# First packs cut to 256 queries, a split weight load and 210 VectorE tiles in a gated attention kernel

## The chip, the cores and the metric

The kernel runs on one core of one Trainium2 chip. The metric is the device time of one execution in microseconds (us), taken as the median of several runs. The engines are called as the profile calls them: PE is TensorE (matrix products), PEld its weight loads, ACT is ScalarE (activations, here the exponentials), DVE is VectorE (elementwise work), POOL is GpSimd and SP is SyncE, which here issues almost all DMAs.

## What is computed

Two attention branches over the same 2048 tokens of width 512 (32 heads of 16) are mixed by a gate per token:

```python
x = A_x
g = _sigmoid((x * gate_w).sum(-1, keepdims=True))
a = _A_ref(x, A_wqkv, A_wo)
b = _B_ref(x, B_wqkv, B_w_phi, B_wo)
return g * a + (1 - g) * b
# A: softmax attention
scores = jnp.einsum("bhqd,bhkd->bhqk", q, k) * (Dh ** -0.5)
o = jnp.einsum("bhqk,bhkd->bhqd", _softmax(scores, axis=-1), v)
# B: linear attention with a feature map of both signs
phi_k = jnp.concatenate([_softmax(pk, axis=-1), _softmax(-pk, axis=-1)], axis=-1)
kv = jnp.einsum("bhsf,bhsd->bhfd", phi_k, v)
o = jnp.einsum("bhqf,bhfd->bhqd", phi_q, kv) / den
```

In B, `pk` and `pq` are k and q times a 16x16 matrix per head (`w_phi`). Branch A needs 32 x 2048 x 2048 exponentials, branch B far fewer.

## The kernel before

**Units and packs.** The scores of A are made transposed: one unit is one head, 128 keys (a key tile) and 512 queries, so a 128x512 block that fills one bank of PSUM. Four heads make a pack (`_unit`, L878): pack p is the key tile p % 16 of group p // 16. A group is four heads and one chunk of 512 queries; there are 32 groups, 512 packs, 2048 units. A unit's scores are one matmul of 32 rows by 512 columns (`_scores`, L906, L913), the four heads of a pack in the four row strips of the array. The last group alone is cut in another way (`_block`, `_parts`): its units are 4 key tiles x 128 queries.

**Who makes the exponentials.** 1840 units go to ACT (`_exp`, L954, L962): it reads a ring of five PSUM banks in turns of three and two banks (`GROUPS`), so 736 activations. The scores of turn k (`_qk`, L930) wait for the exponentials of turn k-2, and for the first two turns for `self.early`: the last reader of each bank that the first projections borrowed (bank 0 and 1: transposes of x, 2: first half of k, 3: first half of q, 4: second half of k). 208 units are taken away from ACT (`SHARES`, L766: how many in each group) and computed on DVE by bit arithmetic and a cubic (`_vector_batch`, L800; `_cubic`, L834), in batches of `NB` = 5 units; `FIRST` and `LAST` give the sizes of the first and last batches. The linear branch uses the same method on DVE (`_b_pair`, L1161). The weighted sum over keys (`_pv`, L969; `_values`, L1024, L1032) runs per pack on PE.

**The start.** `_loads` (L470) issues x in pieces (tokens 0-255, 256-511, then three times 512), the first 128 columns of the q, k and v weights of A, their rest, and then the weights of B in one DMA (`wb`, L506). x is transposed on PE (`_x_transpose`, L601) and copied out (L628). For the first 512 tokens the k and q projections are made in halves of 256 tokens (`_proj_k0` L654, evacuated at L658; `_proj_q0` L669, L675, evacuated twice at L682: once for each side of a pair of heads). The first scores need both halves of q (`b_qT[0]`). V of the first 512 tokens (`_proj_v`, L706, L715) may be made from pack 1 on.

**The linear branch.** `_b_fuse` (L1131) transposes the k part and later the q part of `WB` by DMA (L1133) into one buffer `WT`, multiplies by `wphi` (L1142) and writes the product back (L1147). Then pairs of 128-token tiles follow at due times `K0 + SK * t` for keys and `Q0 + SQ * t` for queries (L1080), in units of packs.

**What sets the order.** Nothing is ordered by hand. Every operation is put into a `Plan` (L66) with an engine, an estimated cost, a priority (`prio`, roughly the pack at which it is due) and a release (`rel`: not before that pack). `order` (L138) runs a greedy list schedule over these estimates, which gives every engine one fixed queue; `now` moves when the scores of a turn are placed, as `_qk` says:

```python
def commit(_):
    plan.now = max(plan.now, (units[-1] + 1) // 4)
```

`emit` writes the queues out with semaphore waits. Each engine then works through its queue in that order, whatever the true times are; SP's queue of DMA issues too. Where PE has room, the plan adds filling matmuls on zeros (`_fill`, L1037, L1041).

Of the kernel before, what the change touches and what calls it, by code (L numbers as in the profile page):

```python
# [10 lines left out]
P = 128  # L11
D = 512
H = 32
DH = 16
TOK = 128
# [335 lines left out]
class _Kernel:  # L351
# [118 lines left out]
    def _loads(self):  # L470
# [4 lines left out]
        self.b_WB, self.b_WoA, self.b_WoB, self.b_wphi, self.b_gw = B(), B(), B(), B(), B()  # L475
# [11 lines left out]
        def load_wa(s, part, eng, prio, lat):  # L487
# [6 lines left out]
        load_x(0, [1], 3.2)  # L494
# [16 lines left out]
    def _consts(self):  # L511
# [30 lines left out]
        self._shared_dma("wphi", parts, self.b_wphi, -5, [z])  # L542
# [3 lines left out]
    def _shared_dma(self, name, parts, buf, prio, deps, cost=0.54):  # L546
        o = self.plan.op("SP", parts, cost * len(parts), name="dma_" + name, prio=prio, deps=deps, lat=8.0)
        buf.writers = [o]


    def _projections(self):
# [3 lines left out]
        self.b_x0, self.b_k0 = [B(), B()], [B(), B()]  # L555
# [45 lines left out]
    def _x_transpose(self, j, half, bank=None):  # L601
# [5 lines left out]
        for t2 in range(2):  # L607
            t = 4 * j + 2 * half + t2
            apart = t2 and bank == 1
# [3 lines left out]
            def tr(e, t=t, t2=t2, job=job):  # L613
                bank = self._bank(job).bitcast(BF16)
                for c in range(4):
# [9 lines left out]
            def copy(e, t0=t0, n=n, job=job, k=t2 - n + 1, apart=apart):  # L625
                out = self.xT[:, :, t0 * TOK:(t0 + n) * TOK].rearrange("p c (t q) -> p t c q", t=n)
                src = self._bank(job).bitcast(BF16).rearrange("p (t c q) -> p t c q", t=2, c=4)[:, k:k + n]
                return e.activation(out, src, ACT.Copy) if apart else e.tensor_copy(out, src)  # L628
            outs.append(op("ACT" if apart else "DVE", copy, 0.5 if apart else 0.068 + 0.27 * n, deps=[mm], name="xtr_ev",
# [24 lines left out]
    def _proj_k0(self, half, bank):  # L654
# [4 lines left out]
                   self.c_dve(256), 2 * half - 2.5, -99, "kproj", [self.b_k0[half]], n=256, bank=bank)  # L659
# [9 lines left out]
    def _proj_q0(self, half, bank):  # L669
# [11 lines left out]
        for side in range(2):  # L681
# [4 lines left out]
            self.b_qT[side].writers.append(o)  # L686
        self.early[bank] = [o]
# [18 lines left out]
    def _proj_v(self, cp, j):  # L706
# [5 lines left out]
        for tt in range(4):  # L712
            def run(e, tt=tt):
                for c in range(4):
# [5 lines left out]
                    rel=due - 20 if cp else -99 if j else 1, acquire=job if tt == 0 else None)  # L720
# [177 lines left out]
    def _parts(self, u):  # L898

        p, i, kt, cp, s = self._unit(u)  # L900
        if self._block(p) is None:
            return [(kt, slice(0, QCH), slice(0, QCH))]
# [27 lines left out]
    def _qk(self, a, b):  # L930
# [19 lines left out]
        if k >= 2:  # L950
            o.slack = self.exps[k - 1]
# [507 lines left out]
```

## Time and profile before

| | |
|---|---|
| median of 3 runs | 848.72 us (848.47 to 849.05) |
| the profiled execution, its own time | 848.98 us |
| span of the profiled execution, first to last instruction | 847.2 us |
| mean granted TensorE clock | 0.999 |
| busy: ACT, DVE, PE | 834.8, 810.5, 810.2 us |
| first exponentials start, last end | 8.90 us, 842.08 us |

The profile comes from one execution. All times in it count from the first instruction of the span, so a time of the profile is smaller than the measured one by what lies around the span (1.78 us in this execution). A group or timeline row names the line of the code, the engine, the operation, output and input by name and shape, the count, and busy time; idle time before it stands with what released the engine. A timeline row starts with the start and the length in us. Activations overlap their neighbours by about a tenth of a microsecond or more, so the pitch between starts, not the length of one, is what counts.

### The profile page before, as it was taken

To read this page: it belongs to the slowest core of one execution; us is meant where nothing else is said; L and a number is where in the kernel's file an instruction comes from. 1 tells how busy PE (TensorE), PEld (TensorE's weight loads), DVE (VectorE), ACT (ScalarE), POOL (GpSimd) and SP (SyncE) were. 2 spreads that over 40 slices of the span, in tenths; PEclk is the share of its full clock that TensorE was granted. 3 is DMA by queue.
4 is the path that set the end of the run, shared out by engine and by line. 5 is a ranking of instruction groups with operands and counts; after the bars stand their busy time and mean duration, and the time that the engine had idled before them with its cause. 6 is when DMAs were issued, how large, how long until landed. Compare 5 with 4: busy or idle time off the path is not lost.

```text
span 847.2 us, 19829 instructions
## 1 busy us (share of the span) xinstructions
PE 810.2 (96%) x8880; PEld 266.0 (31%) x8880; DVE 810.5 (96%) x1029; ACT 834.8 (99%) x741; POOL 7.3 (1%) x14
## 2 busy tenths in 40 slices
PE   9999999999999999999999999999999999999998
PEld 5323233332322322223223223223222222232344
DVE  4589999999999999999999999999999999999996
ACT  6999999999999999999999999999999999999997
POOL 3000000000000000000000000000000000000000
PEclk9999999999999999999999999999999999999999
DMA  9300000000000000002002011001011010030011
GB/s 289 58 10 5 4 2 7 2 6 3 8 2 2 7 2 6 3 2 45 2 7 39 3 24 39 14 2 38 8 36 31 6 29 17 2 57 14 2 33 33
DMA packets 44164, 18.98 MB, mean 22 GB/s; under 512 B 34864, under 2 KB 43568, under 8 KB 44080
## 3 DMA queue, kind: packets, MB, share of 16 engines
q1 hardware_dynamic: 42880, 17.40, 9.2%
q8 instruction: 69, 1.13, 0.5%
q10 hardware_dynamic: 1200, 0.33, 0.2%
q14 instruction: 15, 0.12, 0.1%
HBM read 6.31 MB, written 2.10 MB: 10 GB/s over the span
## 4 chain that ended last, share of the span: by engine, by line
ACT 90%; DVE 5%; PE 3%; DMA 1%; issue 0%; SPq 0%
ACT ET L962 90%; DVE vt L817 1%; PE ps L913 1%; DVE vu L827 1%; DMA phiT<-bq 1%; DMA xn<-in_A_x_dram 0%; DVE vf L842 0%; DVE vf L839 0%; PE ps L616 0%; PE ps L644 0%; DVE vu L843 0%; PE ps L1032 0%; DVE bq L1221 0%; DVE vt L1217 0%; PE ps L1397 0%; PE ps L715 0%
## 5 line engine op out<-in xcount | busy, mean ns | idle before, releaser
L962 ACT ACTIVATE ET<-ps 128x1536 bf16<-128x1536 f32 x736 | 832.3, 1422 | 2.7 <-PE ps L913 2.6
L913 PE MATMUL ps<-qT,kT 32*128 32x512 bf16 (+1 forms) x2240 | 319.9, 365 | 31.2 <-ACT ET L962 23.6
L1041 PE MATMUL ps<-kT,zero 128*32 128x512 bf16 (+1 forms) x3176 | 262.8, 383 | 0.0
L1032 PE MATMUL ps<-ET,V 128*32 128x512 bf16 (+1 forms) x2011 | 196.8, 365 | 0.3 <-DVE T L1061 0.3
L913 PEld LDWEIGHTS ps<-qT,kT 32*128 32x128 bf16 x2240 | 84.3, 91 | 315.1 <-ACT ET L962 239.1
L817 DVE TENSOR_SCALAR vt<-ps 128x512 uint32<-128x512 f32 x208 | 136.1, 679 | 2.2 <-PE ps L913 1.4
L827 DVE SCALAR_TENSOR_TENSOR vu<-vt,vu 128x2560 int16<-128x2560 uint32 (+2 forms) x43 | 117.2, 2726 | 0.2
L1041 PEld LDWEIGHTS ps<-kT,zero 128*32 128x32 bf16 x3176 | 69.5, 94 | 109.7 <-issue 83.2
L842 DVE TENSOR_TENSOR vf<-vf 128x2560 f16<-128x2560 f16 (+2 forms) x59 | 81.2, 1377 | 0.4
L839 DVE TENSOR_SCALAR vf<-vt 128x2560 f16<-128x2560 uint8 (+2 forms) x59 | 81.3, 1378 | 0.2
L1032 PE MATMUL ps<-vu,V 128*32 128x512 bf16 (+1 forms) x229 | 78.1, 362 | 0.0
L1032 PEld LDWEIGHTS ps<-ET,V 128*32 128x32 bf16 x2011 | 54.9, 95 | 62.2 <-issue 37.1
L843 DVE TENSOR_TENSOR vu<-vu,vf 128x2560 f16<-128x2560 f16 (+2 forms) x43 | 61.6, 1434 | 0.2
L644 PE MATMUL ps<-WB,xT 128*128 128x512 bf16 x192 | 55.1, 383 | 0.5 <-DVE vt L817 0.2
L644 PE MATMUL ps<-xT,WA 128*128 128x512 bf16 (+1 forms) x128 | 36.9, 376 | 0.1
L1217 DVE TENSOR_TENSOR vt<-bq,bsum 128x2048 uint32<-128x2048 bf16 x16 | 36.6, 2287 | 0.2
L1221 DVE SCALAR_TENSOR_TENSOR bq<-vt,bq 128x2048 int16<-128x2048 uint32 x16 | 36.5, 2283 | 0.2
L841 DVE TENSOR_SCALAR vu<-vf 128x2560 f16<-128x2560 f16 (+2 forms) x43 | 33.9, 790 | 0.1
L1061 DVE STREAM_TRANSPOSE T<-ps 128x512 f32<-128x512 f32 (+1 forms) x35 | 23.0, 657 | 3.0 <-PE ps L1032 3.0
L1032 PEld LDWEIGHTS ps<-vu,V 128*32 128x32 bf16 x229 | 20.7, 96 | 8.3 <-issue 6.1
L644 PEld LDWEIGHTS ps<-WB,xT 128*128 128x128 bf16 x192 | 14.0, 97 | 25.5 <-issue 13.3
L1174 DVE TENSOR_SCALAR bq<-ps 128x512 bf16<-128x512 f32 x32 | 21.6, 679 | 0.1
(88 smaller groups left out, 409.5 us busy)
## 6 DMA issues: line engine op xcount, KB each, us to landing
qT<-qraw SPq DMA_DIRECT2D x120, 16.0 KB, 1.8
xn<-in_A_x_dram SPq DMA_DIRECT2D x3, 512.0 KB, 6.5
WB<-in_B_wqkv_dram SPq DMA_DIRECT2D x1, 1536.0 KB, 8.8
out_dram<-WB SPq DMA_DIRECT2D x12, 128.0 KB, 1.7
WA<-in_A_wqkv_dram SPq DMA_DIRECT2D x3, 384.0 KB, 7.6
xn<-in_A_x_dram SPq DMA_DIRECT2D x2, 256.0 KB, 3.7
WoA<-in_A_wo_dram SPq DMA_DIRECT2D x1, 512.0 KB, 6.8
WoB<-in_B_wo_dram SPq DMA_DIRECT2D x1, 512.0 KB, 7.8
```

Source lines behind the costliest of these rows:

```text
L644: mm = op("PE", lambda e, c=c: e.matmul(self._bank(job)[:, 0:n], lhs(c), rhs(c), start=(c == 0), stop=(c == 3)), self.c_pe(n), reads=reads ...
L817: parts.append(op("DVE", lambda e, j=j, job=job: e.tensor_scalar(vt[:, j, :], self._bank(job), SCALE * LOG2E * 2.0 ** 24, 2.0 ** 31, op0=A ...
L827: o = op("DVE", lambda e: e.scalar_tensor_tensor(out=flat(vu).bitcast(I16), in0=flat(vt), scalar=2.0 ** -17, in1=flat(vu), op0=ALU.mult, o ...
L839: ("_frac", two, lambda e: e.tensor_scalar(vf, frac, 1 / 256, ROOT, op0=ALU.mult, op1=ALU.add), [b_vt], [b_vf]),
L842: ("_sq", two, lambda e: e.tensor_tensor(vf, vf, vf, ALU.mult), [b_vf], [b_vf]),
L843: ("_cube", two, lambda e: e.tensor_tensor(vu, vu, vf, ALU.mult), [b_vf, b_vu], [b_vu]),
L913: ins = e.matmul(out[u][:, cols], self.kT[32 * i:32 * i + 32, cp, kt * TOK:(kt + 1) * TOK], self.qT[32 * i:32 * i + 32, s, q], start=True, ...
L962: o = plan.op("ACT", lambda e: e.activation(self.ET[:, a % NS:a % NS + n, :], self.ps[:, a % NR:a % NR + n, :], ACT.Exp, scale=SCALE), sel ...
L1032: ins = e.matmul(self._bank(ot)[32 * i:32 * i + 32, 0:width], self.V[:, kt, g8 // 2, v0:v0 + 32], tile[:, cols], start=first and j == 0, s ...
L1041: ins = e.matmul(self._bank(ot)[32 * i:32 * i + 32, lo:QCH], self.zero[:], self.kT[:, 0, lo:QCH], start=False, stop=False, tile_position=( ...
L1217: op("DVE", lambda e: e.tensor_tensor(vt.rearrange("p (g f i) -> p g f i", f=DH, i=4), x, top, ALU.subtract), self.c_dve(n), reads=[b, sel ...
L1221: op("DVE", lambda e: e.scalar_tensor_tensor(out=flat.bitcast(I16), in0=vt, scalar=2.0 ** -17, in1=half, op0=ALU.mult, op1=ALU.add), self. ...
```

## The change

- Packs 0 and 1 are cut in another way: pack 0 is key tiles 0 and 1 with the queries 0-255, pack 1 the same keys with the queries 256-511 (before: key tile 0, then 1, with all 512). Each unit is then two matmuls of 256 columns, in the scores and in the weighted sum. They wait for the half of q that they read (`b_q0[p]`).
- The first two transposed pieces of x are copied out 128 tokens at a time.
- The second half of k (`_proj_k0(1, 4)`) and the transposes of tokens 512-1023 are released at 0, the other transposes at 1, V of the first 512 tokens at pack 4 (`VREL0`).
- The weights of B come in three DMAs: the k part right after x, then `wphi`, then the rest of A's weights, then the v part and the q part. The transpose of the k part has no release any more, priority -6 and an assumed landing time of 2.0 in place of 3.2 us. The gate weights are released at 4.
- The linear keys are due from 11 on every 8.75 packs (before: 22 and 12), the linear queries from 187 on every 14.75 (before: 204 and 18.75).
- DVE takes 210 units (before 208), in other shares per group: 22 in the first eight groups where there were 31; the first batch is one unit, the last two are 4 and 3 (before 2 and 2), and no batch is due before pack 23 (before 12). Lead times and priorities of batches and q projections move (`LEAD`, `QDUE`, `VPRIO`), and the last output tiles are released one pack earlier (`OREL`).

```diff
-    NB, NVU, LEAD = 5, 3, 10
-    QDUE, VPRIO, VREL, TPRIO = 26.0, -10.0, 161.0, -4.0
+    NB, NVU, LEAD = 5, 3, 16
+    QDUE, VPRIO, VREL, TPRIO = 38.0, -24.0, 161.0, -4.0
     KEEP = 14
-    FIRST, LAST = (), (2, 2)
-    OREL = 2
+    EARLY = 23
+    VREL0 = 4
+    FIRST = (1,)
+    LAST = (4, 3)
+    OREL = 1
...
-        load_x(0, [1], 3.2)
+        load_x(0, [1], 3.6)
...
-                                for c in range(4)], self.b_gw, -10, [], 0.78)
-        self.dma("SP", "wb", lambda e: e.dma_start(self.WB[:], self.B_wqkv.rearrange("(c p) j -> p c j", p=P)),
-                 writes=[self.b_WB], prio=-9, lat=8.0)
+                                for c in range(4)], self.b_gw, -4, [], 0.78, 4)
+        WB3 = self.B_wqkv.rearrange("(c p) j -> p c j", p=P)
+        for s, prio, lat in ((1, -46.5, 9.5), (2, -7, 7.0), (0, -5, 7.0)):
+            self.dma("SP", f"wb{s}", lambda e, s=s: e.dma_start(self.WB[:, :, D * s:D * s + D], WB3[:, :, D * s:D * s + D]),
+                     writes=[self.b_WB[s]], prio=prio, lat=lat)
...
-        self._shared_dma("wphi", parts, self.b_wphi, -5, [z])
+        self._shared_dma("wphi", parts, self.b_wphi, -46.2, [z])
...
-            apart = t2 and bank == 1
+            apart = t2 and bank is not None
...
-                    prio=due, rel=1 if j else -99, acquire=pool if apart or t2 == 0 else None)
-            if t2 == 0 and bank != 1:
+                    prio=due, rel=min(j, 2) - 1 if j else -99, acquire=pool if apart or t2 == 0 else None)
+            if t2 == 0 and bank is None:
                 continue
-            t0, n = (t, 1) if bank == 1 else (t - 1, 2)
+            t0, n = (t - 1, 2) if bank is None else (t, 1)
+            own = apart and bank == 1
...
-                   self.c_dve(256), 2 * half - 2.5, -99, "kproj", [self.b_k0[half]], n=256, bank=bank)
+                   self.c_dve(256), 2 * half - 2.5, 0 if half else -99, "kproj", [self.b_k0[half]], n=256, bank=bank)
...
+            if side == 0:
+                self.b_q0[half].writers = [o]
...
-                    rel=due - 20 if cp else -99 if j else 1, acquire=job if tt == 0 else None)
+                    rel=due - 20 if cp else -99 if j else self.VREL0, acquire=job if tt == 0 else None)
...
-    SHARES = (0, 2, 1, 7, 8, 4, 5, 4, 5, 7, 5, 6, 8, 3, 6, 9,
-              8, 10, 7, 6, 8, 10, 7, 8, 7, 8, 8, 7, 2, 14, 11, 7)
+    SHARES = (0, 1, 1, 9, 0, 9, 1, 1, 7, 5, 9, 4, 13, 2, 9, 4,
+              10, 9, 9, 6, 8, 3, 7, 8, 8, 11, 10, 7, 8, 13, 10, 8)
...
-            due = max(units[0] / 4 - self.LEAD, self.NT - 4)
+            due = max(units[0] / 4 - self.LEAD, self.EARLY)
...
         p, i, kt, cp, s = self._unit(u)
+        if p < 2:
+            half = slice(256 * p, 256 * p + 256)
+            return [(j, slice(256 * j, 256 * j + 256), half, half) for j in range(2)]
...
-            for b in (self.b_kT[cp][kt // 4] if cp or kt > 3 else self.b_k0[kt // 2], self.b_qT[s]):
+            for b in (self.b_kT[cp][kt // 4] if cp or kt > 3 else self.b_k0[kt // 2], self.b_q0[p] if p < 2 else self.b_qT[s]):
...
-    K0, SK, Q0, SQ = 22.0, 12.0, 204.0, 18.75
+    K0, SK, Q0, SQ = 11.0, 8.75, 187.0, 14.75
...
-            reads=[self.b_WB], writes=[self.b_WT], prio=due, rel=due - 10, lat=3.2)
+            reads=[self.b_WB[s]], writes=[self.b_WT], prio=-6 if s else due, rel=-99 if s else due - 10, lat=2.0)
...
-                b.readers = list(self.b_WB.readers)
+                b.readers = list(self.b_WB[2].readers)
```

More of the change, by code (lines that the diff above doesn't have):

```diff
@@ L900, in _parts @@
         p, i, kt, cp, s = self._unit(u)
+        if p < 2:
+            half = slice(256 * p, 256 * p + 256)
+            return [(j, slice(256 * j, 256 * j + 256), half, half) for j in range(2)]
         if self._block(p) is None:
-            return [(kt, slice(0, QCH), slice(0, QCH))]
+            return [(kt, slice(0, QCH), slice(0, QCH), slice(0, QCH))]
         b, kq = self._block(p)
-        return [(4 * kq + j, slice(TOK * j, TOK * j + TOK), slice(TOK * b, TOK * b + TOK)) for j in range(4)]
+        return [(4 * kq + j, slice(TOK * j, TOK * j + TOK), slice(TOK * b, TOK * b + TOK), slice(0, TOK)) for j in range(4)]
     def _scores(self, e, units, out):
@@ L911, in _scores @@
             work += [(j, u, i, cp, s, *x) for j, x in enumerate(self._parts(u))]
-        for _, u, i, cp, s, kt, cols, q in sorted(work, key=lambda w: w[0]):
+        for _, u, i, cp, s, kt, cols, q, _ in sorted(work, key=lambda w: w[0]):
             ins = e.matmul(out[u][:, cols], self.kT[32 * i:32 * i + 32, cp, kt * TOK:(kt + 1) * TOK],
@@ L951, in _qk @@
             o.slack = self.exps[k - 1]
+        if units[0] < 8:
+            self.b_qT[0].readers.append(o)
         self.qks.append(o)
@@ L1026, in _values @@
         first = self._acc(p)[1] == 0
[L1027 removed]
         parts = self._parts(4 * p)
[L1029 removed]
+        for j, (kt, cols, _, to) in enumerate(parts):
             for i, tile in src.items():
                 v0 = 17 * (2 * i + g8 % 2)
[L1032 removed]
+                ins = e.matmul(self._bank(ot)[32 * i:32 * i + 32, to], self.V[:, kt, g8 // 2, v0:v0 + 32], tile[:, cols],
                                start=first and j == 0, stop=ot.final[i] is op and j == len(parts) - 1,
```

20 lines of the change are left out of this document (9 added, 11 removed).

## The prediction

> **What bounds the kernel now.** I read the busy shares and the chain of the page first, then the groups of ACT by shape, the chain in order of time and the last activation.
>
> ```profile
> PE 810.2 (96%) x8880; PEld 266.0 (31%) x8880; DVE 810.5 (96%) x1029; ACT 834.8 (99%) x741; POOL 7.3 (1%) x14
> ...
> ACT 90%; DVE 5%; PE 3%; DMA 1%; issue 0%; SPq 0%
> ...
> L962 ACT ACTIVATE ET<-ps 128x1536 bf16<-128x1536 f32 x736 | 832.3, 1422 | 2.7 <-PE ps L913 2.6
> ```
> ```profile
> L962 ACT ACTIVATE ET<-ps 128x1536 bf16<-128x1536 f32 x368 | 601.5, 1635 | 2.7 <-PE ps L913 2.6
> L962 ACT ACTIVATE ET<-ps 128x1024 bf16<-128x1024 f32 x368 | 444.9, 1209 | 0.0
> ```
> ```profile
> 450.97 388.83 ACT ET L962 x344
> ```
> ```profile
> 841.06 1.02 ACT L962 ACTIVATE ET<-ps 128x1024 bf16<-128x1024 f32 x1
> ```
>
> Three engines are near full, but one sets the time. The exponentials are busy 832.3 us, and ACT waited for scores only 2.6 us before them: 1.78 at the first and 0.84 at one more, as the timelines below show. From 8.90 (below) to 842.08 it hardly stops; behind that the last weighted sum, its norm, the projection and the store take 847.2 - 842.08 = 5.1 us. So the span is: start of the first exponential, plus pitch of 736 activations, plus the second wait, plus the tail. The pitch from the long unbroken piece of the chain: 388.83 / 172 = 2.261 us for a turn of three banks and one of two. The mean lengths overlap, but their difference is that of 512 columns, 0.426 us; so a turn of three is (2.261 + 0.426) / 2 = 1.34 us and one of two 0.92 us.
>
> **Fewer units on ACT.** 210 units on DVE leave 1838 on ACT: 367 pairs of turns and one turn of three, 735 activations. One turn of two goes: **-0.92 us**. This holds if DVE can carry two more units and one more batch:
>
> ```profile
> L817 DVE TENSOR_SCALAR vt<-ps 128x512 uint32<-128x512 f32 x208 | 136.1, 679 | 2.2 <-PE ps L913 1.4
> L827 DVE SCALAR_TENSOR_TENSOR vu<-vt,vu 128x2560 int16<-128x2560 uint32 x40 | 112.6, 2814 | 0.2
> L839 DVE TENSOR_SCALAR vf<-vt 128x2560 f16<-128x2560 uint8 x40 | 59.2, 1480 | 0.1
> L842 DVE TENSOR_TENSOR vf<-vf 128x2560 f16<-128x2560 f16 x40 | 59.1, 1479 | 0.1
> L843 DVE TENSOR_TENSOR vu<-vu,vf 128x2560 f16<-128x2560 f16 x40 | 59.1, 1477 | 0.2
> L841 DVE TENSOR_SCALAR vu<-vf 128x2560 f16<-128x2560 f16 x40 | 32.4, 811 | 0.1
> ```
> ```profile
> 8.90:23.41 14.51, 14.06 (x148) 7.43 (x148) 7.40 (x12) 13.66 (x12) 0.61 (x1) 1.00 0.97 294
> 23.41:60.00 36.59, 36.10 (x321) 12.28 (x320) 23.67 (x45) 36.59 (x34) 0.00 (x0) 1.00 0.20 32
> 60.00:100.00 40.00, 39.52 (x396) 13.71 (x397) 39.68 (x49) 40.00 (x36) 0.00 (x0) 1.00 0.02 5
> ```
> ```profile
> 820.00:840.00 20.00, 19.28 (x485) 11.20 (x479) 16.75 (x37) 20.00 (x19) 0.00 (x0) 1.00 0.12 30
> ```
>
> A unit costs DVE 136.1 / 208 = 0.65 us for the bits and (112.6 + 59.2 + 59.1 + 59.1 + 32.4) / 200 = 1.61 us for the rest: two units 4.5 us. A batch more is five instructions whose fixed part I estimate at 0.07 us each (2814 ns for 2560 columns at 0.00107 us a column; lower bound 0, upper bound 0.1): 0.35 us. With ACT some 2 us faster, DVE must find 4.9 + 2 = 6.9 us. In the windows view DVE is full from 60 us on (39.68 of 40), but idle 12.9 us between 23.41 and 60 and 3.3 us in 820-840. The earlier linear keys (due pack 11, not 22; a pack is 1.81 us of ACT, so some 20 us earlier) go into the first gap, which is enough. I count it hidden; its price without that cover is the slower rival below.
>
> **The wait in the start goes.** ACT's second wait is in this stretch:
>
> ```profile
> 18.42 0.82 PE L644 MATMUL ps<-xT,WA 128*128 128x512 bf16 x3
> ...
> 21.37 0.82 PE L644 MATMUL ps<-xT,WA 128*128 128x512 bf16 x3
> ...
> 22.23 0.69 DVE L666 CAST kT<-ps 128x512 bf16<-128x512 f32 x1 [0.60 <-PE ps L644]
> 22.97 0.11 PEld L913 LDWEIGHTS ps<-qT,kT 32*128 32x128 bf16 x5 [0.29 <-DVE kT L666]
> ...
> 23.41 17.27 ACT L962 ACTIVATE ET<-ps 128x1536 bf16<-128x1536 f32 x15 [0.84 <-PE ps L913]
> ```
> ```profile
> 9.55 1.07 PE L715 MATMUL ps<-WA,xT 128*128 128x128 bf16 x16
> ```
>
> The 13th turn reaches key tile 8 and needs k of tokens 1024-1535, copied out at 22.23-22.92. PE is simply full (14.06 of 14.51 us), and what it did before that k was in part not urgent: V of the first tokens at 9.55 (1.07 us), weighted sums, and the q projection for pack 32 (1.1 us, most of it at 18.42). Behind the change V waits for pack 4, the transposes are released sooner, and the weights of that q projection stand behind the new key part and `wphi` on SP, so it can't come so early. That moves at least 2.2 us of PE work behind this k, against 0.84 us of waiting: **-0.84 us** (bounds 0 and -0.84). Next late is PE's backlog of V and weighted sums, for which the 25 slots of exponentials leave room of 25 units, 11 us.
>
> **The first exponential.** Before:
>
> ```profile
> 5.45 1.04 PE L616 MATMUL ps<-iden,xn 128*128 128x128 bf16 x8 [0.25 <-DMA xn<-in_A_x_dram]
> ...
> 6.28 0.73 PE L675 MATMUL ps<-xT,WA 128*128 128x256 bf16 x4
> ...
> 7.49 0.42 DVE L658 CAST kT<-ps 128x256 bf16<-128x256 f32 x1
> ...
> 7.92 0.48 DVE L682 TENSOR_SCALAR qT<-ps,mask 128x256 bf16<-128x256 f32 x1
> 8.36 0.42 DVE L658 CAST kT<-ps 128x256 bf16<-128x256 f32 x1
> 8.46 0.10 PEld L913 LDWEIGHTS ps<-qT,kT 32*128 32x128 bf16 x3 [0.42 <-DVE qT L682]
> 8.46 0.39 PE L913 MATMUL ps<-qT,kT 32*128 32x512 bf16 x3
> 8.70 0.87 DVE L682 TENSOR_SCALAR qT<-ps,mask 128x256 bf16<-128x256 f32 x2
> 8.90 8.23 ACT L962 ACTIVATE ET<-ps 128x1536 bf16<-128x1536 f32 x7 [1.78 <-PE ps L913]
> 9.23 0.09 PEld L913 LDWEIGHTS ps<-qT,kT 32*128 32x128 bf16 x2 [0.67 <-DVE qT L682]
> ```
>
> The first scores wait until 8.40 for the second half of q. With pack 0 on 256 queries they wait for the first half of k, done at 7.91. The finer copies of x do not move that: PE takes the second piece of x at 5.45, ahead of the first q projection at 6.28, as before. So scores at 7.97, exponentials 0.44 later (8.90 - 8.46): 8.41, which is 0.49 earlier. Six matmuls of 256 columns for three of 512 I take as no cost; the bounds are 0 and 0.05.
>
> But the second turn has units 3 and 4 in banks 3 and 4, and bank 4 now holds the second half of k, which is released only when the first scores are placed. PE starts it at about 8.3 (scores' pitch 0.32) and needs 0.6; DVE has the second q copy at 7.92 and the two copies of the other side (0.87 together) ahead of it, 7.92 + 0.44 + 0.87 = 9.23, then 0.42: 9.65. Scores at 9.71, second turn at 10.15, where the first ended its pitch at 8.41 + 1.34 = 9.75. Before, the second turn began at 8.90 + 1.34 = 10.24. What is left of 0.49 is **-0.09 us** (bounds 0 and -0.49).
>
> **The split weight load.** Off the path of ACT unless PE has to wait in its fixed order for `WT`:
>
> ```profile
> WB<-in_B_wqkv_dram SPq DMA_DIRECT2D x1, 1536.0 KB, 8.8
> ...
> WT<-WB SPq DMA_TRANSPOSE x1, 2.5
> ```
> ```profile
> 7.71 3.34 SPq L504 DMA_DIRECT2D gw<-in_gate_w_dram  x4
> ...
> 15.48 0.43 SPq L508 DMA_DIRECT2D WoA<-in_A_wo_dram  x1
> ...
> 25.08 6.16 SPq L1133 DMA_TRANSPOSE WT<-WB  x4
> ...
> 34.82 0.71 PE L1142 MATMUL ps<-wphi,WT 128*128 128x128 bf16 x8
> ```
>
> Before, four transposes were issued from 25.08 to 31.24, landed near 32.5, and PE came to them at 34.82: 2.3 us of margin. Now they stand on SP behind x, `wphi`'s eight issues, A's weights and the two other parts of B's weights. SP had issued as much by 15.48 before, with 3.34 us for the gate's weights in it, which now come later, and with two issues less: some 13 to 14 now (an estimate), so the transposes could land near 14 + 7.4 = 21.4. In the queue all but `WoA` and `WoB` (1 of 6 MB) is ahead of them. The rates below fall off at 22 us; 1 MB at 330 GB/s less is 19 us, and 2.5 behind it 21.5. The plan also assumes 1.2 us less for the landing. So the margin of 2.3 shrinks to about 1 us, or to none if the queue is slower; ACT's own lead, half a turn, covers a little more. I take 0; bounds 0 and +2.
>
> ```profile
> GB/s 0 0 0 166 221 319 349 307 282 352 313 280 321 346 352 348 342 331 325 328 326 326 265 295 389 374 404 416 389 281 279 312 128 270 372 319 120 58 48 27
> ```
> This is the rate from 0 to 24 us in 40 slices. The pieces of x and of A's weights, 0.13 to 0.5 MB each (slices 6 to 19), run at the rates of the 1.5 MB load (from slice 20). The Trainium skill, "DMA: Bandwidth & Descriptors", Rules for kernel authors, advises at least 1 MiB per DMA and to coalesce, which speaks against three parts; its fixed part of about 2 us per DMA would put the last part up to 4 us later if nothing overlapped. This trace does not bear that out for queued loads.
>
> Tail: the steps behind the last exponential wait for each other, not for the released output tiles: 0.
>
> **Sum.** -0.92 - 0.84 - 0.09 = -1.85 us: span 845.35, own time 848.98 - 1.85 = 847.13, and from the median 848.72 - 1.85 = **846.9 us** (-0.22%). The profiled execution lies 0.26 above the median, the same for both. 0.2%, about what a measurement can tell from no change, is 1.7 us: the forecast stands just past it.
>
> **Rivals.**
> 1. *The second turn does not wait*: k's second half is copied out sooner. Then the start gives up to 0.49: 848.72 - 0.92 - 0.84 - 0.49 = 846.5; if PE also takes the first projections ahead of the second piece of x (up to 0.6 us), 845.9. For: DVE has room. Against: the releases as written. 15%.
> 2. *A new wait in the place of the old*: PE stands at `wphi` for `WT`, or its backlog falls into 20-60 us. 1 to 2 us come back: 847.9 to 848.9. For: a margin of 1 us or none, and DMA 97% busy in 8.90-23.41; against: the plan's own due times, and a lead of half a turn. 23%.
> 3. *Slower: DVE's debt.* If the linear keys don't fill the gap of 23-60 us, DVE owes 6.9 us at the end. Only 3.3 us are idle in 820-840, and a last batch of three units instead of two takes 2.3 of these. Then the last weighted sums wait 3.6 to 5.9 us: 846.9 + 3.6 = 850.5, up to 852.8. It decides from the point where less than about 3.6 of the 12.9 us are filled. Against: 20 us of earlier keys. 12%.
>
> **Chances and range.** The forecast has 50%, with a range of its own of 846.5 to 847.4; some two thirds of it lie below 847.0. Faster by over 0.2%: 0.35 + 0.15 = 0.50; within: 0.15 + 0.23 = 0.38; slower: 0.12. The range takes in rivals 1 and 2: 845.9 to 849.0.
>
> **What would show it.** The first exponential at 8.4 and the second turn near 10.15 with 0.4 us of waiting before it; no wait near 23; 735 activations; the first `wphi` product on PE at 22-24 without a wait for DMA; DVE's idle time in 23-60 down by some 7 us or more; the tail still 5.1 us. Wrong would make it: ACT waiting anywhere behind 24, above all beside the `wphi` product and in the last 25 us.

## The result, and the profile after

| | before | after |
|---|---|---|
| median | 848.58 us (848.26 to 850.12, 21 runs) | 847.56 us (846.89 to 848.07, 21 runs) |
| ratio | | 0.9986, 95% interval 0.9979 to 0.9992 |
| profiled execution, its own time | 848.98 us | 847.48 us |
| its span | 847.2 us | 845.7 us |

The change saves 1.0 us (0.12 to 0.14%), where 1.85 was forecast: faster, inside the range, but within the 0.2% that counts as no clear change; the prediction gave that 38%, and 50% to a larger gain. The two profiled executions lie 1.50 us apart; that of before was 0.4 above its median, that of after 0.08 below its own. First the page of the profile after: busy shares, the chain of waits by engine and line, the exponentials.

```profile
PE 814.9 (96%) x8992; PEld 268.1 (32%) x8992; DVE 814.6 (96%) x1037; ACT 834.1 (99%) x740; POOL 7.6 (1%) x14
...
ACT 97%; SPq 1%; POOL 1%; DMA 0%; PE 0%; DVE 0%; issue 0%; POOLq 0%
ACT ET L976 97%; SPq L1146 1%; DMA WT<-WB 0%; SPq L546 0%; POOL V L535 0%; POOL qT L541 0%; SPq L493 0%; SPq L512 0%; POOL V L537 0%; POOL wphi L542 0%; PE ps L1045 0%; DVE xT L1420 0%; PE ps L1410 0%; PE ps L1155 0%; PE ps L925 0%
...
L976 ACT ACTIVATE ET<-ps 128x1536 bf16<-128x1536 f32 x735 | 831.6, 1389 | 2.1 <-PE ps L925 1.9
```

ACT still sets the time, with one activation less. What is new is in the chain: SP's queue (SPq), POOL's clearing of buffers and the transfer into `WT` are links of it now. (The link to POOL is the profile's inference: by the code the loads of `wphi` wait only for the clearing of `wphi`, which ended at 5.04, and the first of them was issued at 6.02.) The chain in order of time says where they join it (start, length, what):

```profile
13.21 3.63 SPq L1146
...
19.50 3.46 DMA WT<-WB
...
23.00 0.40 PE ps L1155 x4
23.40 0.22 PE ps L724 x4
23.62 0.34 PE ps L925 x2
...
23.99 38.63 ACT ET L976 x34
...
62.81 777.60 ACT ET L976 x688
```

Read upwards from 23.99, where ACT starts to run without a stop: it had waited for scores (L925), these stood on PE behind V (L724) and the first product with `wphi` (L1155), this waited for `WT`, which landed at 22.96. Up to 62 us no other wait stands in the chain, and from 62.81 on the pitch is the old one: 777.60 / 344 = 2.2605 us for a pair of turns. ACT's timeline has the waits themselves:

```profile
8.12 1.45 ACT L976 ACTIVATE ET<-ps 128x1536 bf16<-128x1536 f32 x1 [1.43 <-PE ps L925]
9.87 13.91 ACT L976 ACTIVATE ET<-ps 128x1024 bf16<-128x1024 f32 x12 [0.30 <-PE ps L925]
23.99 36.37 ACT L976 ACTIVATE ET<-ps 128x1024 bf16<-128x1024 f32 x32 [0.20 <-PE ps L925]
```

The idle column leaves out about a tenth of a microsecond per wait, since activations overlap, and small waits inside a row. Set against the pitch (1.34 us after a turn of three, 0.92 after one of two), turn by turn, ACT loses 0.41 at its 2nd turn (9.87), 0.33 at the 12th (21.42) and 0.31 at the 14th (23.99), 1.0 in all up to the 41st turn. Before it lost 1.02 at the 13th turn (23.41) and 0.19 at the 38th, 1.0 in all as well. In both kernels at most 0.1 more is lost from the 41st turn to the 701st. So I use the start of the 41st turn below as the mark of what a start is worth: 55.11 before, 54.32 after.

The windows view, in the stretches of the prediction (busy times of PE, PEld, DVE, ACT, POOL, then granted clock, DMA share and GB/s):

```profile
8.90:23.41 14.51, 14.10 (x171) 7.57 (x168) 8.88 (x15) 14.06 (x13) 0.00 (x0) 1.00 1.08 256
23.41:60.00 36.59, 35.86 (x312) 12.14 (x310) 31.58 (x49) 36.39 (x33) 0.91 (x1) 1.00 0.19 48
820.00:840.00 20.00, 19.00 (x448) 10.67 (x446) 13.17 (x28) 20.00 (x19) 0.00 (x0) 1.00 0.06 19
```

DVE's idle time in 23-60 fell from 12.9 to 5.0 us, and in 820-840 it grew from 3.3 to 6.8: two units more were carried with room to spare. PE is as full in the start as before (14.10 of 14.51).

### The profile page after: what moved, and what is told of

It reads as the page before. It is cut to its first block, busy times and chain, and to the rows that moved or that the text cites. A ratio compares the mean times of both kernels' runs of the same rounds, so it can differ in the third digit from the quotient of the medians.

```text
span 845.7 us, 20062 instructions
## 1 busy us (share of the span) xinstructions
PE 814.9 (96%) x8992; PEld 268.1 (32%) x8992; DVE 814.6 (96%) x1037; ACT 834.1 (99%) x740; POOL 7.6 (1%) x14
## 4 chain that ended last, share of the span: by engine, by line
ACT 97%; SPq 1%; POOL 1%; DMA 0%; PE 0%; DVE 0%; issue 0%; POOLq 0%
ACT ET L976 97%; SPq L1146 1%; DMA WT<-WB 0%; SPq L546 0%; POOL V L535 0%; POOL qT L541 0%; SPq L493 0%; SPq L512 0%; POOL V L537 0%; POOL wphi L542 0%; PE ps L1045 0%; DVE xT L1420 0%; PE ps L1410 0%; PE ps L1155 0%; PE ps L925 0%
## 5 line engine op out<-in xcount | busy, mean ns | idle before, releaser
L925 PE MATMUL ps<-qT,kT 32*128 32x512 bf16 (+2 forms) x2248 | 317.1, 364 | 24.2 <-ACT ET L976 18.3
L1054 PE MATMUL ps<-kT,zero 128*32 128x512 bf16 (+1 forms) x3272 | 271.0, 384 | 0.0
L1045 PE MATMUL ps<-ET,V 128*32 128x512 bf16 (+2 forms) x2014 | 194.6, 364 | 0.3 <-ACT ET L976 0.3
L925 PEld LDWEIGHTS ps<-qT,kT 32*128 32x128 bf16 x2248 | 83.7, 91 | 311.0 <-ACT ET L976 225.9
L836 DVE SCALAR_TENSOR_TENSOR vu<-vt,vu 128x2560 int16<-128x2560 uint32 (+4 forms) x44 | 118.5, 2693 | 0.4
L1054 PEld LDWEIGHTS ps<-kT,zero 128*32 128x32 bf16 x3272 | 72.8, 95 | 116.3 <-issue 89.7
L851 DVE TENSOR_TENSOR vf<-vf 128x2560 f16<-128x2560 f16 (+4 forms) x60 | 81.9, 1365 | 0.5
L848 DVE TENSOR_SCALAR vf<-vt 128x2560 f16<-128x2560 uint8 (+4 forms) x60 | 81.9, 1365 | 0.2
L852 DVE TENSOR_TENSOR vu<-vu,vf 128x2560 f16<-128x2560 f16 (+4 forms) x44 | 62.4, 1419 | 0.2
L850 DVE TENSOR_SCALAR vu<-vf 128x2560 f16<-128x2560 f16 (+4 forms) x44 | 34.5, 785 | 0.3
```

What stands on the lines that cost most here:

```text
L836: o = op("DVE", lambda e: e.scalar_tensor_tensor(out=flat(vu).bitcast(I16), in0=flat(vt), scalar=2.0 ** -17, in1=flat(vu), op0=ALU.mult, o ...
L848: ("_frac", two, lambda e: e.tensor_scalar(vf, frac, 1 / 256, ROOT, op0=ALU.mult, op1=ALU.add), [b_vt], [b_vf]),
L851: ("_sq", two, lambda e: e.tensor_tensor(vf, vf, vf, ALU.mult), [b_vf], [b_vf]),
L852: ("_cube", two, lambda e: e.tensor_tensor(vu, vu, vf, ALU.mult), [b_vf, b_vu], [b_vu]),
L925: ins = e.matmul(out[u][:, cols], self.kT[32 * i:32 * i + 32, cp, kt * TOK:(kt + 1) * TOK], self.qT[32 * i:32 * i + 32, s, q], start=True, ...
L1045: ins = e.matmul(self._bank(ot)[32 * i:32 * i + 32, to], self.V[:, kt, g8 // 2, v0:v0 + 32], tile[:, cols], start=first and j == 0, stop=o ...
```

## The experiments

Two theories at first. **A**: the three waits of the start have three causes in the order of work, and each can be moved away by itself. **B**: PE has too much work up to the 40th turn, so what one wait gives up comes back at the next. A third, **C**, came from the first runs: the start is tied to the time at which `WT` lands and to the products with `wphi`, which stand in PE's fixed order among the scores. All edits but those of due times and shares are made in the finished queues: the rest of the order stays word for word, because any other number given to the plan reorders everything behind it. Ratios are to the kernel before, measured beside each.

| run | median us | ratio (95%) | first exp. | lost at turns (us) | 41st turn | last exp. ends |
|---|---|---|---|---|---|---|
| `before_again` | 848.88 (1 run) | | 8.81 | 13th 1.02, 38th 0.19 | 55.02 | 841.98 |
| `after_again` | 847.45 | 0.9983 (0.9974-0.9992) | 7.79 | 2nd 0.41, 12th 0.33, 14th 0.43 | 54.11 | 840.20 |
| `uncut` | 847.69 | 0.9986 (0.9977-0.9995) | 8.12 | 2nd 0.41, 12th 0.31, 14th 0.50 | 54.47 | 840.56 |
| `m_qk1` | 847.54 | 0.9984 (0.9975-0.9993) | 7.79 | 4th 0.62, 5th 0.18, 12th 0.33, 19th 0.16 | 54.25 | 840.33 |
| `m_wphi` | 847.48 | 0.9983 (0.9974-0.9992) | 8.02 | 2nd 0.41, 12th 0.33, 17th 0.16, 19th 0.16 | 54.22 | 840.31 |
| `m_all` | 849.04 | 1.0000 (0.9991-1.0009) | 7.89 | 4th 0.62, 5th 0.18, 14th 1.06, 15th 0.19, 17th 0.34, 19th 0.16 | 55.70 | 841.78 |
| `less_pe` | 847.75 | 0.9988 (0.9979-0.9996) | 7.73 | 2nd 0.41, 15th 0.16, 17th 0.56, 18th 0.20, 19th 0.16 | 54.29 | 840.72 |
| `wtr_first` | 846.87 | 0.9979 (0.9970-0.9988) | 7.76 | 2nd 0.41, 12th 0.33 | 53.51 | 839.62 |
| `wtr_wphi` | 847.46 | 0.9986 (0.9977-0.9994) | 7.69 | 2nd 0.41, 5th 0.18, 12th 0.33, 19th 0.16 | 54.04 | 840.12 |
| `keys22` | 871.19 | 1.0261 (1.0246-1.0277) | 8.03 | 2nd 0.41, 12th 0.33, 40th 0.20; 729th 16.4 | 53.99 | 859.94 |
| `s213` | 846.97 | 0.9978 (0.9969-0.9986) | 8.43 | 2nd 0.41, 12th 0.33, 14th 0.31 | 54.62 | 840.05 |
| `s213_wtr` | 846.44 | 0.9974 (0.9963-0.9984) | 8.13 | 2nd 0.41, 12th 0.33 | 53.91 | 839.31 |

Losses under 0.12 us aren't listed, and of those behind the 41st turn only the one that the text speaks of; the small ones have either sign, so the listed ones differ from the loss at the 41st turn by up to 0.2.

**The same kernels again.** No edit.

> The changed kernel once more, as the yardstick on this chip. Theory A (what ACT loses in the first 24 us is 0.97 us, in three waits that three items in PE's fixed order cause: the second turn's scores behind 16 transposes, the 12th turn's behind the q projection for pack 32, the 14th turn's behind the first wphi product that waits for WT): the three waits stand at the same turns again, together 0.9 to 1.1 us of lost pitch; time 0.8 to 1.2 us under the kernel before. On the start: if PE's speed in the first 6 us is chance, the first eight transposes take 0.62 us in some executions and 1.05 in others, and the first exponential moves between 8.1 and 8.4; if it comes from the change, 0.62 and 8.1 every time.

> The kernel before once more, for a second profile. If PE's speed in the first 6 us is chance, its first eight transposes can take 0.62 us here instead of 1.06, the first exponential starts near 8.6 instead of 8.90, and the span is 0.3 us or so shorter; if it belongs to the kernel, 1.06 and 8.90 come again. ACT loses about 1.0 us of pitch up to the 40th turn either way, in one wait near 23 us.

Both came out alike in the order of their waits, and the first exponential is not a fixed number: 8.12 and 7.79 in two executions of one kernel (8.1 to 8.4 was expected). The 0.33 us that it was earlier were worth 0.2 at the 41st turn, because the 14th turn, behind `WT`, lost 0.43 in place of 0.31. That was the first hint of C.

**First packs whole.** The order is left as it is; only the scores and the weighted sums of packs 0 and 1 use all 512 queries of a key tile, and the first scores wait for both halves of q.

```diff
+            next(x for x in q if x.name == "qk0").deps.append([y for y in p.queues["DVE"] if y.name == "qproj_ev"][1])
+            self.whole = True
...
-        if p < 2:
+        if p < 2 and not self.whole:
```

> Order of every queue as in the changed kernel, but packs 0 and 1 are whole again (key tile 0 and key tile 1 with all 512 queries), and the first scores wait for the second half of q. The first exponential is 0.45 to 0.5 us later than in the changed kernel. Theory B1 (PE works through one fixed order without slack until about 27 us, so what delays it at the first scores stays): the 40th turn and the end are later by the same 0.4 to 0.5 us. Theory B2 (a start gained is given back in the next waits): the waits shrink by as much, the 40th turn stays within 0.15 us and so does the time; then the cut is worth nothing by itself.

PE's rows of this run, and then of the kernel after, from the first q projection to the first scores:

```profile
5.63 0.60 PE L687 MATMUL ps<-xT,WA 128*128 128x256 bf16 x4
...
7.68 0.39 PE L930 MATMUL ps<-qT,kT 32*128 32x512 bf16 x3 [0.58 <-DVE qT L694]
```
```profile
6.12 0.60 PE L682 MATMUL ps<-xT,WA 128*128 128x256 bf16 x4
...
7.67 0.39 PE L925 MATMUL ps<-qT,kT 32*128 32x256 bf16 x6
```

The scores come 1.55 us behind the first q projection with the cut and 2.05 without: the cut is worth 0.50 us at the first exponential. That `uncut` starts its first exponential at 8.12 like the kernel after is chance: its first q projection came 0.49 us sooner. At the end the medians differ by 0.1 to 0.2 (847.69 against 847.45 and 847.56), and the runs overlap. The 14th turn lost 0.50 us in `uncut`, where the kernel after lost 0.31 and 0.43. So what the first packs gain seems to be taken back largely at the 14th turn; with differences as small as these, that is not shown.

**Three moves on PE.** `m_qk1`: the scores of the 2nd turn ahead of the 16 transposes (they no longer wait behind these for k's second half, which gets a pooled bank). `m_wphi`: the first product with `wphi` behind the scores of the 14th turn. `m_all`: both, and the q projection for pack 32 behind the scores of the 13th turn.

```diff
-                self._proj_k0(1, 4)
+                self._proj_k0(1, None)
...
+            move([at("qk1")], at("xtr", 4))
```
```diff
+            move([at("wphi")], q[q.index(at("qk13")) + 1])
```
```diff
+            move([at("qproj", n) for n in range(2, 6)], q[q.index(at("qk12")) + 1])
```

> Order as in the changed kernel, but the second turn's scores stand ahead of the 16 transposes of tokens 512-1023, and the second half of k is projected in a pooled bank, so that these scores do not wait for its copy. Theory A (three separate waits, each with its own price): no wait at the second turn, ACT 0.41 us earlier from there on, 0.4 us less in all. Theory B (PE is full until 24 us, so what is saved ahead comes back at the next late scores): the second turn's wait goes, the 12th turn waits 0.4 us more, the time stays within 0.1 us of the changed kernel.

> Order as in the changed kernel, but the first wphi product stands behind the 14th turn's scores instead of ahead of them. Theory A and B alike: PE's wait for WT at 23 us no longer holds scores, ACT's wait of 0.20 us (0.24 of pitch) at the 14th turn goes: 0.2 to 0.25 us less. A third theory (the late WT is not what holds ACT): ACT waits as long for something else and the time stays.

> All three moves: second turn's scores ahead of the transposes with the second half of k in a pooled bank, q projection for pack 32 behind the 13th turn's scores, first wphi product behind the 14th turn's. Theory A: no wait of ACT in the first 24 us, 0.9 to 1.0 us less than the changed kernel, so 1.8 to 2.0 under the kernel before. Theory B (PE is full): at most half of that, 0.2 to 0.5 us, and a new wait of 0.4 us or more between 20 and 40 us.

Each move takes its own wait away. In the two single moves others of about the same sum come; in `m_all` the new ones are 1.5 us more than the old. So A fails as it stood. In `m_qk1` ACT's timeline shows the 2nd turn on time and the 4th late:

```profile
7.79 3.73 ACT L986 ACTIVATE ET<-ps 128x1536 bf16<-128x1536 f32 x3 [1.20 <-PE ps L935]
12.03 9.33 ACT L986 ACTIVATE ET<-ps 128x1024 bf16<-128x1024 f32 x8 [0.51 <-PE ps L935]
```

In `m_all` the time is that of the kernel before. The rows around the 14th turn, PE, DVE and ACT in order of time:

```profile
21.85 1.04 PE L663 MATMUL ps<-xT,WA 128*128 128x512 bf16 x4
...
22.92 0.69 DVE L718 CAST qraw<-ps 128x512 bf16<-128x512 f32 x1 [2.19 <-PE ps L663]
...
23.67 0.62 PE L736 MATMUL ps<-WA,xT 128*128 128x128 bf16 x8 [0.24 <-DVE qraw L718]
...
24.23 0.39 PE L937 MATMUL ps<-qT,kT 32*128 32x512 bf16 x2
...
24.65 2.56 ACT L988 ACTIVATE ET<-ps 128x1024 bf16<-128x1024 f32 x2 [0.93 <-PE ps L937]
```

The projection now ends at 22.89, DVE copies it out at 22.92, only then is the bank free into which V (L736) goes, and the scores of the 14th turn stand behind V. So here it isn't the amount of PE's work that makes ACT late, but an operation in front of the scores that waits for a copy on DVE or for a transfer. `m_wphi` shows the same at the products: with the first of them moved back, the last one comes to its bank too early: at 26.12 PE has stood 0.49 us for DVE's copy of `WB`.

**Less work on PE.** This kernel leaves out two of the four matmuls of the q projection for pack 32 and half of two blocks of V, 1.3 us of PE, and has the first product with `wphi` behind the scores of the 14th turn.

```diff
+            proj = [x for x in q if x.name == "qproj"][3:5]
+            proj += [x for x in q if x.name == "vproj"][1:3] + [x for x in q if x.name == "vproj"][9:11]
+            for x in proj:
+                q.remove(x)
...
+            q.insert(q.index(k13) + 1, w)
```

> Order as in the changed kernel with the first wphi product behind the 14th turn's scores, and less work on PE: two of the four matmuls of the q projection for pack 32 and half of the V blocks of tokens 512-1535 are left out (1.3 us of PE), so parts of q and V are wrong. Theory B (PE is full until about 27 us and its amount of work sets where ACT is at the 40th turn): the waits at the 12th turn and behind it go, only the 0.41 us at the second turn stay; the 40th turn 0.5 to 0.6 us earlier relative to the first, the time 0.5 us less. Theory A (single waits): only what the shorter q projection held, about 0.2 to 0.3 us. If neither the work nor the order of PE binds, 0.

The 41st turn started at 54.29, as in the kernel after and in `m_wphi` (54.22), from which this run differs only by the work left out. The 12th turn lost nothing here, so the shorter projection did bring ACT forward there; 0.56 us at the 17th turn took it back. B falls for this order: with 1.3 us less to do, PE came to the same wait earlier. Its rows:

```profile
23.00 0.40 PE L1167 MATMUL ps<-wphi,WT 128*128 128x128 bf16 x4 [0.46 <-DMA WT<-WB]
24.18 0.40 PE L1167 MATMUL ps<-wphi,WT 128*128 128x128 bf16 x4 [0.24 <-DVE WB L1172]
26.05 0.40 PE L1167 MATMUL ps<-wphi,WT 128*128 128x128 bf16 x4 [0.49 <-DVE WB L1172]
```

PE again gets on at 23.00, when `WT` is there (23.00 after, 23.16 in `uncut`), whatever it had done before, and then waits for the copies of the products. That is C. No run takes work off PE with `WT` early, so whether PE's work would count then is open.

**`WT` earlier.** The decisive run: on SP the four transposes are issued ahead of the loads of B's v and q parts, 1 MB, and nothing else moves. `wtr_wphi` has the move of `m_wphi` as well.

```diff
+            q = p.queues["SP"]
+            w = at("dma_wtr1")
+            q.remove(w)
+            q.insert(q.index(at("dma_wb2")), w)
```

> The changed kernel with one move on SP's queue: the four transposes of WB into WT are issued ahead of the loads of B's two other parts (V and query), not behind them; every other queue as it is. Theory C (the start up to the 40th turn is anchored by WT, which lands at 22.7 to 23.1 and on which PE stands in its fixed order): 1 MB less ahead of WT, some 2 to 3 us at the rate of the trace, so WT lands near 20; the first product with wphi starts at 22.6 without a wait for DMA, the 14th turn loses nothing instead of 0.31 to 0.43, the 41st turn starts 0.3 to 0.4 us earlier (53.7 to 53.9 against 54.1 to 54.5), time 847.1 to 847.3. Theory B (PE has too much to do before turn 40, whatever the order): the 0.4 us come back at the next turns, 41st turn at 54.1 to 54.3, time 847.5. Rival: V and query part of B land later, PE then stands at B's V near 31: up to 1 us more, 848.

> The same move on SP, and on PE the first product with wphi stands behind the scores of the 14th turn. Theory C: with WT early neither the 14th turn nor those near the 17th and 19th (0.16 each when only the product was moved) lose time; only what is lost at the 2nd and 12th turn, 0.7, is left; 41st turn at 53.5 to 53.8, time 847.0 to 847.2. Theory B: 41st turn at 54.1 to 54.3, 847.5.

`wtr_first` is 0.6 to 0.7 us faster than the change, more than expected; its slowest run (847.19) is faster than the fastest of `after_again` (847.21). Its timeline of SP and PE, then its chain and ACT:

```profile
13.32 5.24 SPq L1152 DMA_TRANSPOSE WT<-WB  x4
18.60 1.13 SPq L518 DMA_DIRECT2D WB<-in_B_wqkv_dram  x2
```
```profile
22.17 0.39 PE L1161 MATMUL ps<-wphi,WT 128*128 128x128 bf16 x4
...
22.71 0.39 PE L931 MATMUL ps<-qT,kT 32*128 32x512 bf16 x2
```
```profile
21.07 40.77 ACT ET L982 x36
...
62.03 777.60 ACT ET L982 x688
```
```profile
7.76 1.45 ACT L982 ACTIVATE ET<-ps 128x1536 bf16<-128x1536 f32 x1 [1.34 <-PE ps L931]
9.51 20.69 ACT L982 ACTIVATE ET<-ps 128x1024 bf16<-128x1024 f32 x18 [0.30 <-PE ps L931]
```

The transposes are issued in 5.24 us (7.64 after) and the last one lands at 19.81 (22.96 after). The product runs at 22.17 in its turn with no wait, and the 14th turn loses nothing. The long piece starts 0.78 us earlier than after (62.03 for 62.81): 0.36 of that from the first exponential of this execution, 0.42 from the wait that is gone and small ones behind it. Against `after_again`, whose first exponential was at nearly the same time (7.79), the 41st turn is 0.60 earlier. The two parts of B that now come later were not missed. `wtr_wphi` is a miss: 847.46 where C gave 847.0 to 847.2. Its PE waits at the last product, though `WT` was long there:

```profile
25.05 0.40 PE L1165 MATMUL ps<-wphi,WT 128*128 128x128 bf16 x4
25.93 0.40 PE L1165 MATMUL ps<-wphi,WT 128*128 128x128 bf16 x4 [0.49 <-DVE WB L1170]
```

From the first exponential to the 41st turn `wtr_wphi` takes 0.59 us longer than `wtr_first`. Only half of that, 0.29, comes behind the 14th turn, where the products are. The other 0.30 comes before, most of it at the 4th and 5th turn, ahead of all that was moved: at 9.91 PE had waited 0.29 us for a piece of x. So C needs a second half: the products take banks that DVE frees one copy after another, and the plan's spacing of them is right if `WT` is on time. `m_wphi` had broken the second half while it mended the first. The price of that half, some 0.3 us, rests on these single profiles.

**Later linear keys.** The due times of the linear branch as before, with 210 units.

```diff
-    K0, SK, Q0, SQ = 11.0, 8.75, 187.0, 14.75
+    K0, SK, Q0, SQ = 22.0, 12.0, 204.0, 18.75
```

> The changed kernel with the linear keys and queries due as before (22 and 12, 204 and 18.75); the plan orders all the rest anew around that. Rival 3 of the prediction, the debt of VectorE: DVE idles 5 us or more longer between 23 and 60 us, owes it at the end, and ACT or the last weighted sums wait: 4 to 8 us slower than the changed kernel, 3 or more slower than the kernel before. If DVE is not what binds, the time stays within 1 us of the changed kernel.

22.4 us slower than before and 23.6 slower than after, far beyond the 4 to 8 expected. The windows view, ACT's longest wait, and the granted clock in 40 slices of the span (in tenths):

```profile
23.41:60.00 36.59, 35.13 (x308) 12.34 (x312) 23.81 (x48) 36.59 (x35) 0.61 (x1) 1.00 0.23 48
...
100.00:200.00 100.00, 95.72 (x1008) 33.94 (x1016) 94.59 (x118) 100.00 (x90) 0.00 (x0) 1.00 0.02 4
200.00:400.00 200.00, 188.78 (x2050) 55.74 (x2061) 192.42 (x241) 199.99 (x179) 0.00 (x0) 1.00 0.03 7
```
```profile
849.96 1.45 ACT L976 ACTIVATE ET<-ps 128x1536 bf16<-128x1536 f32 x1 [16.35 <-PE ps L1045]
```
```profile
PEclk9999999999999999999999999999999999999958
```

DVE was busy 23.8 us in 23-60 (31.6 after), 94.6 in 100-200 (99.7) and 192.4 in 200-400 (199.4): some 20 us of its time went by unused, and 16.4 us of waiting at the 729th turn, smaller waits behind it and a tail that is 4.2 us longer (9.44) stand at the end. So DVE's debt comes back at the end, and in size not far from one to one. It isn't shown that all of it is debt: in the last two slices, from 826 us on, the clock granted to PE fell to about 0.5 and 0.8, and DVE there waited for PE again and again, so a part is PE's slower pace. The edit moves the linear queries too, so it isn't the keys alone. It also shows the start without products among the early scores: the 14th turn loses nothing.

**One activation less again.** 213 units on DVE, alone and with the early transposes.

```diff
-    SHARES = (0, 1, 1, 9, 0, 9, 1, 1, 7, 5, 9, 4, 13, 2, 9, 4,
-              10, 9, 9, 6, 8, 3, 7, 8, 8, 11, 10, 7, 8, 13, 10, 8)
+    SHARES = (0, 1, 1, 9, 0, 9, 1, 1, 8, 5, 9, 4, 13, 2, 10, 4,
+              10, 9, 9, 6, 8, 3, 6, 9, 8, 10, 11, 7, 9, 12, 11, 8)
```

> The changed kernel with 213 units on DVE in place of 210, spread otherwise over the groups; the order of the start is the same. One turn of three banks less on ACT: -1.34 us if DVE can carry three units more (3 x 2.26 = 6.8 us); DVE is idle 5.0 us in 23-60 and 6.8 in 820-840, so this is near its limit. If DVE carries it: 846.1 to 846.3. If DVE's debt shows, as with the later linear keys: a wait of ACT or of the last weighted sums in the last 100 us, 847.5 to 850.

> Both moves that helped: 213 units on DVE and the transposes into WT ahead of B's two other parts. If they are independent (one takes 0.3 to 0.7 us out of the start, the other one turn of three less 0.8 us of waits beyond turn 200): 41st turn at 53.5 to 53.9, loss at the 14th turn none, time 846.2 to 846.5. If DVE's debt takes the gain (ACT comes to the same late batches earlier by what the start saved): the waits beyond turn 200 grow from 0.8 by as much, 846.8 to 847.0.

`s213` lies between its two cases: the turn of 1.34 us is gone, but 0.8 us are lost between the 41st and the 701st turn (0.1 after), in small waits of 0.1 to 0.7. `s213_wtr` is the sum of both, 846.44 us, as expected if they are independent, and the fastest kernel here: 2.2 us below the kernel before, twice the gain of the change. Its losses beyond the 41st turn are the same 0.8.

## Why the prediction was right or wrong

Term by term, in the two profiled executions (us):

| term | forecast | measured | how |
|---|---|---|---|
| a turn of two less | -0.92 | -0.89 | 41st turn to last exponential's end, 786.97 to 786.08 |
| start of the 2nd turn | -0.09 | -0.38 | 10.25 to 9.87 |
| the wait near 23 | -0.84 | -0.41 | 2nd to 41st turn, 44.86 to 44.45 |
| tail | 0 | +0.18 | 5.10 to 5.28 |
| sum | -1.85 | -1.50 | span 847.18 to 845.68 |

In medians it is -1.02, since the profiled execution of before lay 0.40 above its median and that of after 0.08 below. That part of the difference belongs to no term.

- **The turn less: right.** 735 activations, the pitch unchanged.
- **DVE's room: right**, and the price of the rival was too low. DVE filled 7.9 us of its gap (7 or more was said). The fixed part of a batch was too small: no row gives the 0.00107 us a column from which 0.07 us per instruction came. The rows of the same instructions in the kernel after, with 512 and with 2560 columns (680 and 2814 ns, 426 and 1480, 294 and 815), leave 0.15 to 0.16 us each, so by my estimate 0.8 us a batch in place of 0.35, and 7.3 to find in place of 6.9. `keys22` shows the mechanism of rival 3, with 22.4 us where 2 to 4 were worked out: I had priced the debt of two units and ACT's lead, not all the linear work that the later due times leave undone.
- **The first exponential: right in its mechanism**, 0.50 against 0.49 by `uncut`, and the second turn's wait of 0.41 against 0.40. That it came at 8.12 and not 8.41 is chance of the first 6 us (below), and so is 0.29 of the 0.38 us in the table: without that luck the sum of these two profiles would be about 1.2. I counted the second turn as the end of the start's gain; the waits behind it were not in that sum.
- **The wait near 23: the step that failed.** The wait itself went, as forecast: k of tokens 1024-1535 was copied out at 19.20 (22.23 before), and the 13th turn lost nothing. By pitch that is 1.02 us, not 0.84, which was the idle column's figure. What failed is that the whole of it was booked as gained: I took PE to be full, found 2.2 us of its work that would move behind that k, and did not look for what stands in front of the neighbouring scores. 0.33 and 0.31 us came back at the 12th and the 14th turn. Of the work that I named, the q projection for pack 32 did move behind that k (18.42 before, 20.03 after), and V of the first tokens did not (9.55 before, 11.77 after). But behind that k the q projection stood right in front of the 12th turn's scores, and the first product with `wphi` in front of the 14th's. `less_pe` took 1.3 us off PE and gained nothing in the end.

```profile
19.20 0.69 DVE L673 CAST kT<-ps 128x512 bf16<-128x512 f32 x1 [2.33 <-PE ps L651]
...
20.03 1.02 PE L651 MATMUL ps<-xT,WA 128*128 128x512 bf16 x4
...
23.00 0.40 PE L1155 MATMUL ps<-wphi,WT 128*128 128x128 bf16 x4 [0.41 <-DMA WT<-WB]
```

  The first row is the copy of that k; the other two are PE's operations ahead of the 12th and the 14th turn in the kernel after, where 0.33 and 0.31 us are lost. For the 14th `wtr_first` shows the cause. For the 12th two runs agree: `m_all`, which moves the projection, and `less_pe`, which halves it, both lose nothing there. Neither gained from it: `m_all` lost 1.06 at the 14th turn and `less_pe` 0.56 at the 17th, so what the 12th turn's wait costs in the end is not shown.
- **The margin of `WT`: a bound that I saw and left out.** I put its landing near 21.4 and took 0 of a range of 0 to +2; it landed at 22.96, and 0.31 to 0.43 us is its price. SP came to the transposes at 13.21, as estimated (13 to 14). But they took 9.75 us to land in place of the 7.4 of the kernel before: the two loads ahead of them landed at 19.50 and 20.93, where I had put their end at 19, and the first transpose at 21.45, right behind. In `wtr_first`, issued at 13.32 without these loads ahead, the last one landed at 19.81. How much of the 3.15 us is the loads' data and how much SP's slower issue (below), no run separates. This is rival 2, "a new wait in the place of the old", with its first place named rightly and its price of 1 to 2 us too high. With the 12th turn's wait it is why the time fell between the forecast's own range and that rival.
- **The tail** is longer by 0.13 to 0.2 us in every run with 210 units and the early keys (5.24 to 5.30; before 5.10 and 5.11). The part from the last exponential to DVE's last copy is even 0.1 shorter, so the rest lies behind the last copy, 2.24 to 2.53 us. I looked for no cause, and it stays open.

## What to carry to other kernels

A wait that ends last hides the next one: before counting it as gained, list which operation with a foreign wait (a transfer, a copy that frees a bank) stands in front of the following scores in the engine's fixed order, and when that wait ends. An engine that is 97% full in a stretch need not be the bound of the stretch: taking work away from it is a cheap test, which says only what binds in the order as it stands. When a load is cut into parts so that one can come early, its consumer's issue must be moved past the other parts too: here that one move was worth 0.6 us, more than half as much as the whole change.

## What the runs showed of the hardware

SP's queue as a resource. The kernel after, from x to the transposes (start, length of the issues, count):

```profile
3.91 2.07 SPq L512 DMA_DIRECT2D WB<-in_B_wqkv_dram  x1
6.02 4.47 SPq L546 DMA_DIRECT2D wphi<-in_B_w_phi_dram  x8
10.53 1.53 SPq L493 DMA_DIRECT2D WA<-in_A_wqkv_dram  x3
12.11 1.06 SPq L512 DMA_DIRECT2D WB<-in_B_wqkv_dram  x2
13.21 7.64 SPq L1146 DMA_TRANSPOSE WT<-WB  x4
```

A 512 KB load takes SP 0.5 us to issue (1.06 / 2), but 2.07 behind the pieces of x; eight issues of 2 KB take 4.47; a transpose takes 1.26, but 3.63 where it is the first behind 1 MB of loads. In `wtr_first`, without that 1 MB, four took 5.24, but the load ahead of them took 1.70 in place of 0.51. In `after_again` the first transpose took 2.51 and a load ahead of it 1.36, and in the kernel before, 1.35 us after the last load had landed (23.73), the first took 2.23. So the loads ahead are not the whole reason; what holds such an issue is not shown.

PE in its first microseconds. The same 16 transposes of x took 2.16 us in `s213`, 1.64 in `wtr_first` and 2.01 in the second execution of before:

```profile
4.14 2.16 PE L622 MATMUL ps<-iden,xn 128*128 128x128 bf16 x16
...
6.10 0.93 PE L682 MATMUL ps<-xT,WA 128*128 128x256 bf16 x4
```
```profile
4.14 1.64 PE L628 MATMUL ps<-iden,xn 128*128 128x128 bf16 x16
5.76 0.60 PE L688 MATMUL ps<-xT,WA 128*128 128x256 bf16 x4
```

The work up to there is the same in both; the first exponential was at 8.43 and 7.76. The Trainium skill, "TensorE: Matmul & The Clock Gate", Part 1, describes a clock that starts at half speed and is released after an activity window of some 3.4 us that runs free of the kernel's start, so that the point of release differs from run to run. The rows agree: 0.93 and 0.60 us for the same four matmuls, at times that differ between executions. The profile's granted clock does not show it: it reads 1.00 from 4 to 8 us in both.

That isn't the only scatter. In the kernel after and in `after_again` the transposes ran at the same speed, but the second piece of x came 0.46 us earlier in the second:

```profile
5.43 0.62 PE L622 MATMUL ps<-iden,xn 128*128 128x128 bf16 x8 [0.62 <-DMA xn<-in_A_x_dram]
```
```profile
4.97 0.62 PE L622 MATMUL ps<-iden,xn 128*128 128x128 bf16 x8 [0.42 <-DMA xn<-in_A_x_dram]
```

Over all runs from the kernel after on, the first exponential lies between 7.69 and 8.43, so one profile gives a start to no better than some 0.7 us, which here is as much as the terms in question.
